# Top-k attention and SoLU feed-forward on one core: a new place table with named PSUM units, small work moved to GpSimd, and the verdict read earlier

## The chip, the core and the metric

The kernel runs on one core of a Trainium2 chip. The metric is the device time of one execution in microseconds, the median of three runs: 1089.7 us (1087.85 to 1089.91). In the profile PE is TensorE, PEld its weight loads, DVE is VectorE, ACT is ScalarE, POOL is GpSimd and SP is SyncE, whose queue issues nearly all DMAs.

## The reference

For 8 batches of 8 heads, with 576 queries and keys of 64 elements, attention keeps the 32 largest scores of each query row:

```python
scores = scale * np.matmul(q, k.transpose(0, 1, 3, 2))
kth = np.partition(scores, -top_k, axis=-1)[..., -top_k:-top_k + 1]
mask = scores >= kth
attn = exp(where(mask, scores, -1e9) - rowmax); attn = attn / (sum + 1e-9); out = attn @ v
```

The result, 4608 tokens of 512 elements, goes through a feed-forward block:

```python
h = x @ w_in                      # 512 -> 1024
sm = exp(h - max) / (sum + 1e-9)
solu = h * sm
ln = (solu - mean(solu)) / np.sqrt(var(solu) + 1e-06) * g_ln
return ln @ w_out                 # 1024 -> 512
```

The weights arrive as 64-bit floats.

## The kernel before, in words

The attention is cut into 32 steps (`steps_of`, L451). A step takes 512 query rows: in the two outer batches (0 and 7) one chunk of 128 queries for all four head pairs, in the others two chunks for two head pairs. Nine rows of work (`j` from 0 to 8) make up a step: eight of 128 queries by 576 keys and one for the queries' tails (64 queries of two heads).

A step runs through these stages. `load_q`, `prep_q` and `prep_qc` fetch the queries and turn them on PE; `load_t` fetches the tails of queries and keys, and `prep_k` turns the keys with their tails. `estimate`, `length`, `root` (L1935) and `gained` guess a threshold for each row from lengths. `scores` (L1980, L1969) multiplies on PE, and `evac` (L1995) copies the result out of PSUM on ScalarE. `count0` and `count1` count the elements above the threshold. From the count, `count_off` (L2106, L2109, GpSimd) makes `far`, the square of how far the count is from 32. On DVE `nearest` (L2064), `best` (L2075) and `merged` (L2092) sort the 16 elements nearest to the threshold; `which` (L2115) compares a table of 16 odd squares, `ranks`, with `far`, `chosen` (L2122) multiplies the sorted elements by the result, and `chosen_sum` (L2125) adds them up: this picks the 32nd largest score. `exps` takes the exponentials on ScalarE, `keep` (L2148) zeroes what lies under the 32nd and sums the rest into `den_all`, `inverse` (L2156, L2160) takes the reciprocals. `transpose_p` and `transpose_last` turn the kept exponentials on PE, `copy_p` (L2249) copies them out, `attn_v` (L2301) and `attn_t` (L2316, L2323) multiply by the values, and `copy_v` (L2338, L2345) scales on DVE.

When a batch's tokens are ready, each of 36 token tiles of 128 rows runs `mm1` (L2356), `hexp` (L2367), `solu` (L2372 to L2379), `square` (L2385), `spread` and `ln` (L2391 to L2398, GpSimd), `transpose_ln`, `copy_ln`, `mm2` (L2420), `store` (L2427: a copy to SBUF) and `send` (L2431: the DMA out). In `solu` the row of exponentials is divided by its sum (the reciprocal `rs` is a scalar operand), and the mean is made by scaling `nmu`.

The 16 weight pieces of 512 KB are brought to 32 bits in the early part: `load_w`, `w_bits` and `w_corr` (DVE), `w_sum` (L1687 to L1692, PE, with three extra matmuls each), `w_copy`. Late in the run they are read once more and tested (`w_again`, `w_exp`, `w_check`). `w_passed` and `w_verdict` (L2451 to L2454) count how many rows met all conditions and write the flag `bad`. After the fast path every engine loads that flag into a register (L2501) and branches (L2503): where the flag is set, a slow general path would run. It does not run for these inputs.

What sets the order is a table written out by hand: `PLACES` gives each piece of work an integer, and `arranged` (L479) sorts the pieces by it. PE, ScalarE, DVE and GpSimd run their instructions in exactly that order; semaphores make each wait for its data and for its buffer. PSUM is handed out by one pool of four units of two banks (`ps_big`, L1536, tag `big`): each of `scores`, `transpose_p`, `attn_v`, `mm1` and the like takes a unit, which is free again when its last reader is through. Which of the four units a take gets is decided by the pool.

## Time and profile before

| | |
|---|---|
| median of three runs | 1089.7 us (1087.85 to 1089.91) |
| profiled execution | 1089.88 us, span 1088.1 us |
| PE busy | 1038.2 us, 95% |
| DVE busy | 998.0 us, 92% |
| ACT busy | 997.0 us, 92% |
| POOL busy | 241.9 us, 22% |

The span runs from the first to the last instruction; the profiled execution's own time lies 1.78 us above it. A busy time is the union of an engine's instructions. PE's matmuls are pipelined and their ends are modelled, so a busy PE is not PE at its peak. "Granted clock" (PEclk) is the TensorE clock that the chip allowed, as a share of 2.4 GHz.

### The profile page before, as it was taken

The numbers are of one execution on the slowest core, as the hardware profiler recorded it, in microseconds if no ns is written. First come the engines' busy times: TensorE is split into PE (matmuls) and PEld (weight loads), VectorE is DVE, ScalarE is ACT, GpSimd is POOL, SyncE is SP. The second block draws the span as 40 slices with busy tenths as digits, with TensorE's granted clock in tenths as the row PEclk, the third lists the DMA queues.
The fourth block names the chain that finished last, engine by engine and source line by source line (L and its number), as shares of the span: only waits on it lengthen the run. The fifth ranks groups of instructions, "written<-read, shape, count | busy, mean of one in ns | idle before, by whom it ended". The sixth has DMA issues, their size and how long they took to land.

```text
span 1088.1 us, 23584 instructions
## 1 busy us (share of the span) xinstructions
PE 1038.2 (95%) x8367; PEld 592.6 (54%) x8367; DVE 998.0 (92%) x2945; ACT 997.0 (92%) x1979; POOL 241.9 (22%) x401
## 2 busy tenths in 40 slices
PE   6858999999999999999999999999999999999997
PEld 3335556554555555565555555565555556565553
DVE  4999998999999999999999999999999999998800
ACT  6968998999999999999999999999999999998722
POOL 1301221313034122122223122221312213220100
PEclk9979999999999999999999999999999999999999
DMA  9510111112111121111210122111310111134301
GB/s 261 160 59 11 41 41 53 44 51 51 52 44 51 36 69 53 32 51 41 73 52 22 51 51 63 41 45 33 79 54 21 41 37 49 54 119 137 108 11 33
DMA packets 108807, 64.54 MB, mean 59 GB/s; under 512 B 87940, under 2 KB 96392, under 8 KB 108680
## 3 DMA queue, kind: packets, MB, share of 16 engines
q1 hardware_dynamic: 107608, 62.68, 20.4%
q8 instruction: 68, 1.11, 0.4%
q14 instruction: 59, 0.48, 0.1%
q10 hardware_dynamic: 1072, 0.26, 0.1%
HBM read 53.35 MB, written 9.57 MB: 58 GB/s over the span
## 4 chain that ended last, share of the span: by engine, by line
PE 57%; DVE 22%; ACT 16%; issue 2%; POOL 1%; DMA 1%; ACTq 0%; DVEq 0%
PE h_ps L2356 16%; PE o_ps L2420 15%; PE om L2301 8%; PE s_ps L1980 6%; DVE w L2064 5%; DVE w L2075 5%; DVE E L2148 4%; PE tp_p L1782 4%; ACT sg L2043 3%; DVE junkv L2000 3%; ACT X L1995 2%; ACT PT L2249 2%; ACT E L2100 2%; PE om L2316 2%; PE s_ps L1969 2%
## 5 line engine op out<-in xcount | busy, mean ns | idle before, releaser
L2420 PE MATMUL o_ps<-w_out,lnT 128*128 128x512 f32 x576 | 261.5, 599 | 1.8 <-ACT lnT L2413 1.0
L2356 PE MATMUL h_ps<-w_in,xTm 128*128 128x512 f32 x512 | 229.8, 598 | 2.7 <-DVE xTm L2338 2.2
L2075 DVE MAX8 w<-w 128x8 f32<-128x288 f32 x576 | 224.7, 445 | 0.0
L2043 ACT ACTIVATE sg<-X,t 128x576 int8<-128x576 f32 x256 | 200.5, 812 | 7.7 <-DVE t L2028 5.5
L2064 DVE SCALAR_TENSOR_TENSOR w<-X,al,sg 128x576 f32<-128x576 f32 x256 | 202.4, 814 | 0.2
L2148 DVE SCALAR_TENSOR_TENSOR E<-X,kth,E 128x576 f32<-128x576 f32 x256 | 201.2, 820 | 1.0 <-ACT E L2100 0.3
L2420 PEld LDWEIGHTS o_ps<-w_out,lnT 128*128 128x128 f32 x576 | 105.4, 190 | 120.9 <-issue 112.6
L2356 PEld LDWEIGHTS h_ps<-w_in,xTm 128*128 128x128 f32 x512 | 94.2, 190 | 110.0 <-issue 105.9
L2000 DVE TENSOR_SCALAR_CACHE_REDUCE junkv<-X,t 128x576 uint8<-128x576 f32 x188 | 148.4, 805 | 6.1 <-ACT X L1995 4.5
L2100 ACT ACTIVATE E<-X 128x1152 f32<-128x1152 f32 x128 | 152.5, 1209 | 0.0
L1995 ACT ACTIVATE X<-s_ps 128x768 f32<-128x768 f32 x192 | 147.2, 839 | 2.0 <-PE s_ps L1980 1.2
L1980 PE MATMUL s_ps<-kT,qT 64*128 64x384 f32 (+1 forms) x1024 | 144.9, 418 | 2.3 <-ACT PT L2249 0.7
L2301 PE MATMUL om<-PT,vm 128*64 128x256 f32 (+3 forms) x1280 | 136.8, 365 | 3.7 <-DVE solu L2375 1.9
L2249 ACT COPY PT<-tp_p 128x1024 f32<-128x1024 f32 x128 | 130.6, 1042 | 0.6 <-PE tp_p L1782 0.3
L1980 PEld LDWEIGHTS s_ps<-kT,qT 64*128 64x128 f32 x1024 | 85.3, 187 | 40.8 <-issue 5.8
L2301 PEld LDWEIGHTS om<-PT,vm 128*64 128x64 f32 x1280 | 82.7, 138 | 45.2 <-ACT PT L2249 4.1
L1935 POOL TENSOR_TENSOR zs<-zs,phalf 128x9 f32<-128x9 f32 x32 | 67.6, 2113 | 137.8 <-DVE zs L1927 118.4
L1782 PE MATMUL tp_p<-ident,E 64*128 64x64 f32 x2048 | 81.4, 224 | 3.9 <-DVE E L2148 1.5
L1782 PEld LDWEIGHTS tp_p<-ident,E 64*128 64x128 f32 x2048 | 72.4, 138 | 21.5 <-issue 5.7
L2036 POOL TENSOR_SCALAR tt<-t 128x9 f32<-128x9 f32 x32 | 18.4, 576 | 288.2 <-DVE t L2028 244.7
L2043 ACT ACTIVATION_READ_ACCUMULATOR sg<-X,t 128x1 f32 x256 | 60.2, 235 | 0.0
L2391 POOL TENSOR_SCALAR var<-var 128x1 f32<-128x1 f32 x36 | 11.0, 306 | 213.0 <-ACT e_sb L2385 207.7
(153 smaller groups left out, 1576.3 us busy)
## 6 DMA issues: line engine op xcount, KB each, us to landing
km<-in_k_dram SPq DMA_DIRECT2D x32, 256.0 KB
vm<-in_v_dram SPq DMA_DIRECT2D x32, 256.0 KB
out_dram<-osb SPq DMA_DIRECT2D x32, 256.0 KB
...
```

The source lines that it names most:

```text
L1782: nc.tensor.transpose(out[:, a, :], part(rows), ident[rows, rows])
L1980: nc.tensor.matmul(out=s[:, n, m * part : (m + 1) * part], lhsT=queries_of(i, t)[hd, :], rhs=kT[hd, k0 : k0 + part], start=True, stop=True,)
L1995: nc.scalar.activation(out=x, in_=s, func=AF.Copy, scale=scale)
L2000: nc.vector.tensor_scalar(out=junk, in0=x_of(i, j), scalar1=st[i][t][:, j : j + 1], scalar2=None, op0=ALU.is_ge, op1=ALU.add, accum_out=co ...
L2043: nc.scalar.activation(out=d["sg", j], in_=x_of(i, j), func=AF.Sign, scale=-(1.0 + 2.0**-23), bias=d["t1"][:, j : j + 1], accum_out=column ...
L2064: nc.vector.scalar_tensor_tensor(out=w, in0=x_of(i, j), scalar=d["al"][:, j : j + 1], in1=d.pop(("sg", j)), op0=ALU.subtract, op1=ALU.mult,)
L2075: nc.vector.max(w8[:, j, 8 * half : 8 * half + 8], w[:, half * SH : (half + 1) * SH])
L2100: nc.scalar.activation(out=d["E", t][:, 0 : x2_of(i, t).shape[1]], in_=x2_of(i, t), func=AF.Exp)
L2148: nc.vector.scalar_tensor_tensor(out=e, in0=x_of(i, j), scalar=d["kth"][:, j : j + 1], in1=e, op0=ALU.is_ge, op1=ALU.mult, accum_out=den_a ...
L2301: nc.tensor.matmul(out=o[h * D : (h + 1) * D, cols], lhsT=vm[:, h, c, :], rhs=pt[:, h * NM + c, :], start=(c == 0), stop=False,)
L2356: nc.tensor.matmul(out=h[:, half, :], lhsT=x[:, c, :], rhs=w_in[:, c, half * 512 : (half + 1) * 512], start=(c == 0), stop=(c == NP - 1),)
L2420: nc.tensor.matmul(out=o, lhsT=d["lnT"][:, c, :], rhs=w_out[:, c, :], start=(c == 0), stop=(c == NF - 1),)
```

## The change

- **Places.** Nearly all places are new. Among the first: a weight piece and the first queries are loaded before keys; `prep_q` and `w_bits` stand before `prep_k`.
- **PSUM units.** The pool of four units is replaced by four pools of one. The string `UNITS` has a character for each take, in the order of the table; `0` to `3` name the unit, `a` to `d` the same four for the takes that only 64-bit weights need.
- **Undivided rows.** `solu` multiplies by the exponentials without the division by their sum. Since a row's scale cancels in the normalization, only the small constant under the root has to be scaled to match: `norm`, three operations on one column on GpSimd, makes that constant and the mean. `square` works on rows scaled by the width, `spread` adds the constant, and the width's power goes into the copy of `g_col`.
- **Ranks on GpSimd.** `which` subtracts `far` from the ranks on GpSimd into a buffer of its own, and `chosen` on DVE tests for zero and multiplies in one instruction.
- **One reciprocal.** `keep` writes its sums in the order in which `inverse` needs them, which is then one instruction.
- **Last tokens and verdict.** The last two token tiles change places. `w_verdict` stands before the last but one half of `mm2`, the flag is loaded just ahead of the last `store`, and the last `send` goes out by ScalarE's queue.

```diff
@@ -468,4 +468,18 @@
+UNITS = (
+    "0b23a1230bc0310231ac3012da123a1231a2badb03120231032120132013cb0210213021321031230123010231"
+    "020320130312032023021321321013120210210321030230131013213213210230123132103210231022031031"
...
+    "103102310230123210"
+)
...
 def order_of_tokens(B):
+    order = [(b, t) for b in range(B) for t in range(NM + b % 2)]
+    return order[:-2] + order[:-3:-1]
...
-    "mm1", "hexp", "solu", "square", "spread", "ln", "transpose_ln", "copy_ln", "mm2", "store", "send",
+    "mm1", "hexp", "solu", "norm", "square", "spread", "ln", "transpose_ln", "copy_ln", "mm2", "store", "send",
...
     "load_k": [
-        0, 1000, 2000, 10400, 36774, 37774, 109467, 119254, 120254, 141054, 208848, 209848, 237397,
...
+        4900, 5900, 10800, 11800, 25850, 26850, 114754, 115754, 119182, 147008, 201104, 210489,
...
-    "load_t": [0, 46136, 142054, 235497, 373816, 520839, 620166, 756840],
+    "load_t": [0, 27850, 148008, 235241, 368859, 514159, 616708, 754927],
     "prep_k": [
-        5218, 7029, 7709, 13812, 108817, 118604, 118987, 140404, 208198, 208581, 234464, 234847,
...
+        10443, 10826, 14811, 15194, 114104, 114487, 118532, 146358, 199863, 209839, 232591, 232974,
...
     "load_q": [
-        3550, 11400, 20200, 29974, 44886, 81424, 124601, 150273, 180902, 220584, 247601, 286809,
...
+        1950, 16700, 35200, 36200, 52123, 84924, 123039, 168135, 187716, 202104, 237481, 272752,
...
     "prep_q": [
-        6558, 19138, 31858, 38406, 80511, 141115, 175499, 179290, 226194, 239634, 288397, 291891,
...
+        4958, 19931, 44587, 44054, 84717, 155005, 175355, 178198, 203970, 254465, 283693, 288241,
...
     "root": [
-        17967, 26053, 40014, 91752, 126126, 153797, 183630, 224113, 249956, 288384, 300353, 327150,
...
+        20469, 27791, 68532, 94941, 127341, 169283, 188046, 202653, 238056, 274637, 296233, 332100,
...
     "mm2": [
...
-        [1058331, 1061873],
...
+        [1054813, 1058355],
     "store": [
...
-        1050731, 1058484, 1065568,
...
+        1047213, 1054966, 1062050,
     "load_w": [
-        4550, 6500, 8450, 12400, 14350, 16300, 18250, 22374, 24324, 26274, 34824, 40524, 42936,
...
+        0, 2950, 6900, 8850, 12800, 14750, 18250, 21950, 23900, 29750, 37200, 39150, 50173, 57175,
...
     "w_bits": [
-        8770, 11064, 13989, 16620, 19315, 23644, 24706, 36870, 32134, 30997, 39887, 45708, 57859,
...
+        4220, 7170, 11120, 13514, 17890, 20274, 25709, 27596, 33137, 34279, 54561, 45672, 57265,
...
-    "w_verdict": [1065308],
+    "w_verdict": [1051221],
@@ -1486,2 +1506,3 @@
     bad: bass.AP,
+    failed: list,
 ):
@@ -1535,3 +1556,3 @@
     )
-    ps_big = ctx.enter_context(tc.tile_pool(name="ps_big", bufs=4, space=PS))
+    ps_big = ctx.enter_context(tc.tile_pool(name="ps_big", bufs=1, space=PS))
 
@@ -1619,4 +1640,6 @@
 
+    units = (str("0123abcd".index(u) % 4) for u in UNITS if w_wide or u in "0123")
+
     def two_banks(name):
-        return ps_big.tile([P, 2, 512], F32, tag="big", name=name)
+        return ps_big.tile([P, 2, 512], F32, tag="big" + next(units), name=name)
 
@@ -1636,3 +1659,5 @@
     def copy_g():
-        nc.scalar.copy(out=g_col, in_=gain["tp"][:, 0:NF])
+        nc.scalar.activation(
+            out=g_col, in_=gain["tp"][:, 0:NF], func=AF.Copy, scale=float(DFF) ** 1.5
+        )
 
@@ -2113,6 +2138,6 @@
         d = st[i]
-        hot = d["hot"] = d["by"][:, 0, :, :]
-        nc.vector.tensor_tensor(
+        hot = d["hot"] = small.tile([P, NT, 16], F32, tag="hot", name="hot", bufs=1)
+        nc.gpsimd.tensor_tensor(
             out=hot, in0=ranks.unsqueeze(1).broadcast_to([P, NT, 16]),
-            in1=d["far"].unsqueeze(2).broadcast_to([P, NT, 16]), op=ALU.is_equal,
+            in1=d["far"].unsqueeze(2).broadcast_to([P, NT, 16]), op=ALU.subtract,
         )
@@ -2121,3 +2146,6 @@
         d = st[i]
-        nc.vector.tensor_tensor(out=d["hot"], in0=d["hot"], in1=d["by"][:, 3, :, :], op=ALU.mult)
+        nc.vector.scalar_tensor_tensor(
+            out=d["hot"], in0=d["hot"], scalar=0.0, in1=d["by"][:, 3, :, :],
+            op0=ALU.is_equal, op1=ALU.mult,
+        )
 
@@ -2147,5 +2175,6 @@
         e = p_of(i, j)
+        row = j if j == 2 * NM else j % 2 * NM + j // 2
         nc.vector.scalar_tensor_tensor(
             out=e, in0=x_of(i, j), scalar=d["kth"][:, j : j + 1], in1=e,
-            op0=ALU.is_ge, op1=ALU.mult, accum_out=den_all[:, i, j : j + 1],
+            op0=ALU.is_ge, op1=ALU.mult, accum_out=den_all[:, i, row : row + 1],
         )
@@ -2155,7 +2184,3 @@
         rden = columns(i, "rden")
-        nc.vector.reciprocal(
-            rden[:, 0 : 2 * NM].rearrange("p (h t) -> p t h", h=2),
-            den_all[:, i, 0 : 2 * NM].rearrange("p (t h) -> p t h", h=2),
-        )
-        nc.vector.reciprocal(rden[:, 2 * NM : NT], den_all[:, i, 2 * NM : NT])
+        nc.vector.reciprocal(rden, den_all[:, i, :])
 
@@ -2353,3 +2378,3 @@
         x = d["x"]()
-        h = once(d, "h", lambda: ps_big.tile([P, 2, 512], F32, tag="big", name="h_ps"))
+        h = once(d, "h", lambda: two_banks("h_ps"))
         for c in range(NP):
@@ -2370,4 +2395,2 @@
 
-        rs = small.tile([P, 1], F32, tag="rs", name="rs")
-        nc.vector.reciprocal(rs, d["sum"])
         d["solu"] = p2.tile([P, DFF], F32, tag="solu", name="solu")
@@ -2375,7 +2398,16 @@
         nc.vector.scalar_tensor_tensor(
-            out=d["solu"], in0=h_of(d), scalar=rs, in1=d["e"], op0=ALU.mult, op1=ALU.mult,
+            out=d["solu"], in0=h_of(d), scalar=1.0, in1=d["e"], op0=ALU.mult, op1=ALU.mult,
             accum_out=nmu,
         )
-        nc.vector.tensor_scalar(
-            out=nmu, in0=nmu, scalar1=-1.0 / DFF, scalar2=None, op0=ALU.mult
+
+    def norm(d):
+
+        less = d["less"] = small.tile([P, 1], F32, tag="less", name="less")
+        nc.gpsimd.tensor_scalar(
+            out=less, in0=d["sum"], scalar1=1e-6 * DFF**3, scalar2=0.0, op0=ALU.mult, op1=ALU.add
+        )
+        nc.gpsimd.tensor_tensor(out=less, in0=less, in1=d["sum"], op=ALU.mult)
+        mean = d["mean"] = small.tile([P, 1], F32, tag="mean", name="mean")
+        nc.gpsimd.tensor_scalar(
+            out=mean, in0=d["nmu"], scalar1=-1.0 / DFF, scalar2=0.0, op0=ALU.mult, op1=ALU.add
         )
@@ -2385,3 +2417,4 @@
         nc.scalar.activation(
-            out=d["e"], in_=d["solu"], func=AF.Square, bias=d["nmu"], accum_out=d["var"]
+            out=d["e"], in_=d["solu"], func=AF.Square, scale=-float(DFF), bias=d["nmu"],
+            accum_out=d["var"],
         )
@@ -2390,5 +2423,3 @@
         var = d["var"]
-        nc.gpsimd.tensor_scalar(
-            out=var, in0=var, scalar1=1.0 / DFF, scalar2=1e-6, op0=ALU.mult, op1=ALU.add
-        )
+        nc.gpsimd.tensor_tensor(out=var, in0=var, in1=d["less"], op=ALU.add)
         d["rstd"] = small.tile([P, 1], F32, tag="rstd", name="rstd")
@@ -2398,3 +2429,3 @@
         nc.gpsimd.tensor_scalar(
-            out=d["solu"], in0=d["solu"], scalar1=d["nmu"], scalar2=d["rstd"],
+            out=d["solu"], in0=d["solu"], scalar1=d["mean"], scalar2=d["rstd"],
             op0=ALU.add, op1=ALU.mult,
@@ -2425,2 +2456,7 @@
     def store(d):
+        if d is tokens[-1]:
+            failed.append(nc.values_load(
+                bad[0:1, 0:1], min_val=0, max_val=1,
+                skip_runtime_bounds_check_because="a comparison's result",
+            ))
         d["osb"] = p1.tile([P, DM], F32, tag="osb", name="osb")
@@ -2429,4 +2465,5 @@
     def send(d):
+        queue = nc.scalar if d is tokens[-1] else nc.sync
         for rows, dst in d["stores"]:
-            nc.sync.dma_start(out=dst, in_=d["osb"][rows, :])
+            queue.dma_start(out=dst, in_=d["osb"][rows, :])
 
@@ -2439,3 +2476,3 @@
             (zk_all, 1e-12, ALU.is_gt), (den_all, 1.0, ALU.is_ge), (den_all, 1e15, ALU.is_le),
-            (sum_all, 1.0, ALU.is_ge), (sum_all, 1e30, ALU.is_le), (w_ok, 128.5, ALU.is_le),
+            (sum_all, 1.0, ALU.is_ge), (sum_all, 1e12, ALU.is_le), (w_ok, 128.5, ALU.is_le),
             (end_all, 0.5, ALU.is_gt),
@@ -2481,3 +2518,3 @@
         keep, inverse, spread_r, copy_s, turn_r, copy_r, rd_out, rd_in, transpose_p, copy_p, transpose_last, copy_last, attn_v, attn_t,
-        copy_v, mm1, hexp, solu, square, spread, ln, transpose_ln, copy_ln, mm2, store, send, load_g, turn_g,
+        copy_v, mm1, hexp, solu, norm, square, spread, ln, transpose_ln, copy_ln, mm2, store, send, load_g, turn_g,
         copy_g, load_w, w_bits, w_corr, w_sum, w_copy, w_gain, w_again, w_exp, w_check, w_passed,
@@ -2499,6 +2536,5 @@
     bad = keep.tile([1, 1], I32, tag="bad", name="bad")
-    fast_path(tc, *args, bad)
-    failed = nc.values_load(bad[0:1, 0:1], min_val=0, max_val=1,
-                            skip_runtime_bounds_check_because="a comparison's result")
-    with tc.If(failed > 0):
+    failed = []
+    fast_path(tc, *args, bad, failed)
+    with tc.If(failed[0] > 0):
         general_path(tc, *args)
```

## Rows read from the trace of the kernel before

**Rows 1.** The page, part 1: busy us, share of the span, instructions

```profile
PE 1038.2 (95%) x8367; PEld 592.6 (54%) x8367; DVE 998.0 (92%) x2945; ACT 997.0 (92%) x1979; POOL 241.9 (22%) x401
```

**Rows 2.** The page, part 4: shares of the chain that ended last

```profile
PE 57%; DVE 22%; ACT 16%; issue 2%; POOL 1%; DMA 1%; ACTq 0%; DVEq 0%
```

**Rows 3.** Timeline of POOL: start us, us, engine, line, operation; first `root`

```profile
22.71 2.01 POOL L1935 TENSOR_TENSOR zs<-zs,phalf 128x9 f32<-128x9 f32 x1 [20.36 <-DVE zs L1927]
```

**Rows 4.** Timeline of ACT: three of the 36 `store` copies

```profile
164.63 0.75 ACT L2427 COPY osb<-o_ps 128x512 f32<-128x512 f32 x1
...
206.48 0.60 ACT L2427 COPY osb<-o_ps 128x512 f32<-128x512 f32 x1
...
1080.45 0.59 ACT L2427 COPY osb<-o_ps 128x512 f32<-128x512 f32 x1 [6.28 <-PE o_ps L2420]
```

**Rows 5.** Groups of DVE by line: count, busy us, mean ns, idle before

```profile
L2148 DVE SCALAR_TENSOR_TENSOR E<-X,kth,E 128x576 f32<-128x576 f32 x256 | 201.2, 820 | 1.0 <-ACT E L2100 0.3 <-issue 0.2
...
L2115 DVE TENSOR_TENSOR by<-ranks,far 128x144 f32<-128x144 f32 x32 | 9.7, 302 | 0.0
...
L2372 DVE RECIPROCAL rs<-sum_all 128x1 f32<-128x1 f32 x36 | 5.6, 156 | 16.9 <-ACT e_sb L2367 16.6
...
L2379 DVE TENSOR_SCALAR nmu<-nmu 128x1 f32<-128x1 f32 x36 | 5.5, 154 | 1.3
...
L2160 DVE RECIPROCAL rden<-den_all 128x1 f32<-128x1 f32 x32 | 3.6, 112 | 0.0
```

**Rows 6.** One line each: ns min/median/max, first and last start

```profile
L2109 POOL TENSOR_TENSOR far<-far x32: 201/518/1175, 50.1 to 1005.3; 128x9 f32<-128x9 f32 x32
...
L2148 DVE SCALAR_TENSOR_TENSOR E<-X,kth,E x256: 796/814/1680, 71.8 to 1025.1; 128x576 f32<-128x576 f32 x128
```

**Rows 7.** Timeline of POOL, then of DVE, 690 to 720 us

```profile
693.56 0.60 POOL L2109 TENSOR_TENSOR far<-far 128x9 f32<-128x9 f32 x1
702.24 0.26 POOL L2391 TENSOR_SCALAR var<-var 128x1 f32<-128x1 f32 x1 [8.08 <-ACT e_sb L2385]
...
703.13 0.31 DVE L2122 TENSOR_TENSOR by<-by 128x144 f32<-128x144 f32 x1
```

**Rows 8.** Waits of PE: waited for, us in total, times, longest

```profile
PE om L2301 <- DVE solu L2375: 1.9, 1, 1.9
```

**Rows 9.** Stretches: us, busy us by engine (instructions), PEclk, DMA share, GB/s

```profile
55.00:60.00 5.00, 0.00 (x0) 0.00 (x0) 5.00 (x11) 4.99 (x14) 0.00 (x0) 0.50 0.00 0
70.00:75.00 5.00, 2.72 (x28) 1.65 (x27) 5.00 (x15) 3.24 (x6) 0.00 (x0) 1.00 0.28 107
180.00:182.00 2.00, 2.00 (x18) 1.68 (x16) 2.00 (x7) 0.72 (x2) 1.11 (x2) 0.50 0.29 83
```

**Rows 10.** Timeline of PE, 176 to 188 us

```profile
179.16 4.07 PE L2301 MATMUL om<-PT,vm 128*64 128x128 f32 x32 [1.86 <-DVE solu L2375]
...
185.46 1.92 PE L2301 MATMUL om<-PT,vm 128*64 128x128 f32 x32
```

**Rows 11.** Timeline of PE, then of DVE, from the start

```profile
9.30 0.37 PE L1782 MATMUL tp_k<-ident,qk_tails 64*128 64x64 f32 x1 [2.39 <-DMA qk_tails<-in_k_dram]
...
11.44 0.17 DVE L1856 TENSOR_TENSOR stats<-sums,heads 128x6 bf16<-128x6 f32 x1 [9.22 <-ACT kT L1834]
```

**Rows 12.** Stretches of the start, columns as in rows 9

```profile
0.00:10.00 10.00, 1.40 (x11) 0.96 (x11) 1.19 (x8) 1.49 (x2) 1.79 (x37) 1.00 0.94 181
10.00:20.00 10.00, 10.00 (x63) 5.77 (x63) 5.91 (x14) 9.30 (x31) 0.00 (x0) 1.00 1.06 324
```

**Rows 13.** Flag load L2501, branch L2503: ns min/median/max, first and last start

```profile
L2501 SPq TENSOR_LOAD <-bad x1: 841/841/841, 1082.3 to 1082.3; - x1
...
L2503 SPq EVENT_SEMAPHORE  x8: 17/17/17, 1086.1 to 1086.7; - x8
L2503 ACTq COMPARE_BRANCH  x1: 54/54/54, 1081.4 to 1081.4; - x1
...
L2503 ACTq EVENT_SEMAPHORE  x1: 17/17/17, 1085.7 to 1085.7; - x1
```

More of the change, by code (lines that the diff above doesn't have):

```diff
@@ new lines @@
+        [99561, 108898],
+        [136125, 146234],
+        [158968, 171847],
+        [193719, 187748],
+        [225810, 221745],
+        [258577, 262835],
+        [287807, 287116],
+        [319273, 313968],
+        [341060, 347114],
+        [375505, 374721],
+        [394747, 404333],
+        [433489, 422728],
+        [461074, 454078],
+        [487820, 486491],
+        [511202, 530372],
+        [540945, 557314],
+        [584352, 599472],
+        [614624, 625790],
+        [642165, 651531],
@@ L1175 @@
[L1175 to L1181 removed]
+        [79248, 70794],
+        [100489, 109753],
+        [140208, 146918],
+        [159683, 173991],
+        [196779, 188257],
+        [227369, 222218],
+        [261004, 263314],
+        [289217, 287589],
+        [331756, 314426],
+        [343175, 347821],
+        [380868, 375287],
+        [395641, 407160],
@@ new lines @@
+        [438124, 423117],
+        [461768, 454462],
+        [489483, 487106],
+        [517584, 533829],
+        [543006, 557698],
+        [585187, 600016],
+        [619356, 626947],
+        [643425, 652285],
+        [677583, 685877],
+        [705391, 720086],
+        [736646, 752993],
+        [769067, 779376],
+        [803785, 813463],
+        [843237, 851534],
+        [861094, 866315],
+        [896755, 902651],
+        [914529, 921776],
+        [941932, 949178],
+        [971559, 991104],
@@ new lines @@
+        [204661, 207452],
+        [228989, 226695],
+        [272545, 278767],
+        [291317, 288602],
+        [336466, 341609],
+        [370200, 368422],
+        [387129, 395790],
+        [413815, 416019],
+        [450800, 449022],
+        [471445, 469667],
+        [506146, 508350],
+        [535068, 537859],
+        [581118, 596771],
+        [609072, 611276],
+        [637109, 639313],
+        [666754, 664976],
+        [695597, 693339],
+        [721435, 723639],
+        [749580, 757818],
@@ new lines @@
+        [294754, 294200],
+        [339942, 344856],
+        [373544, 374006],
+        [394151, 398338],
+        [419145, 419607],
+        [454255, 453793],
+        [475147, 474740],
+        [511560, 512022],
+        [538537, 540687],
+        [587948, 599319],
+        [614383, 614845],
+        [641915, 642377],
+        [670621, 670204],
+        [700277, 696538],
+        [726241, 726703],
+        [753454, 760366],
+        [784784, 785246],
+        [829641, 836229],
+        [859132, 864401],
@@ new lines @@
+        [437525, 434090],
+        [441069, 444504],
+        [488421, 475964],
+        [501741, 498306],
+        [541546, 549361],
+        [558845, 553766],
+        [566491, 563056],
+        [616051, 619486],
+        [628438, 631982],
+        [674105, 677540],
+        [686535, 681945],
+        [727402, 732445],
+        [736918, 744725],
+        [791286, 786124],
+        [803391, 799956],
+        [812825, 807905],
+        [870022, 866587],
+        [877001, 873566],
+        [909753, 913188],
```

864 lines of the change are left out of this document (382 added, 482 removed), and 576 rows, old and new, of the table PLACES.

## The prediction

> **What bounds the kernel now.** I read the busy shares first, then the chain of waits, then single starts. TensorE is busy 1038.2 of 1088.1 us, VectorE 998.0, ScalarE 997.0 [rows 1]: three engines are nearly full, so no one of them can be relieved alone. The chain that ended last lies 57% on PE, 22% on DVE, 16% on ACT [rows 2]. The reader should see from this that work taken from DVE is worth at most about a fifth of its length, and that PE, from which the change takes nothing, goes on setting the end.
>
> The next view is that of single starts. Each engine runs its instructions in the order of the place table. The integers in it behave as nanoseconds: the first square root of GpSimd (`root`, place 17,967) starts at 22.71 [rows 3]; the copies `store` with places 159,179, 197,741 and 1,065,568 start at 164.63, 206.48 and 1080.45 [rows 4]. The lag of start behind place is 4.74, 5.45, 8.74 and 14.88 us. So the trace tells of a table with three separate losses: 4.74 us at the start, 3.29 us in one jump between 164 and 206, and 6.85 us spread over the rest (under 1% of the span). A new table is not believed for its own sake; I take over its differences only with these measured losses, and bound them where a row can.
>
> **The change part by part.**
>
> *Order and DVE work.* Off DVE go the reciprocal `rs` (36 x 156 ns = 5.6 us), the scaling of `nmu` (36 x 154 ns = 5.5), the comparison with `ranks` (32 x 302 ns = 9.7) and one of two reciprocals (32 x 112 ns = 3.6) [rows 5]: 24.4 us. `chosen` keeps its 144 elements and one pass. Worth from both sides: 24.4 us if DVE alone set the time, nothing if PE did; by DVE's 22% of the chain, 5.4. The new table puts the last `store` at 1,062,050 in place of 1,065,568, which is 3.52 us earlier. I take 3.5, which lies between nothing and 5.4. PE keeps every matmul; the end of the table is again mm1, transposes and mm2 without a gap.
>
> *GpSimd.* It gains 32 subtractions of 144 elements and 36 x 3 operations on one column (`norm`); `spread` keeps its two. A 9-element operation there takes 201 to 1175 ns [rows 6]. I take 0.6 us for a subtraction and 0.25 us for a column operation: 32 x 0.6 + 108 x 0.25 = 46 us beside 242 us busy, 27% of the span. What hides the subtraction: in a typical step `far` is ready at 694.16 (693.56 + 0.60) and its first reader's successor `chosen` starts at 703.13 on DVE, with GpSimd idle for 8.08 us between [rows 7]. What hides `norm`: ScalarE's square of the same token runs beside it, and the next GpSimd operation, `var`, is the one that waits for that square [rows 7]. If this cover went, a token's `ln` would come 0.8 us later, at a PE that is then in another token's matmuls. Both engines share a cost: `keep` on DVE has a median of 814 ns, a mean of 820 and a maximum of 1680 [rows 5, 6], so meetings with GpSimd cost DVE (820 - 814) x 256 = 1.5 us in all. With 140 more operations on about 400 I charge 1 us, bounds 0 and 5.
>
> The Trainium skill ("SBUF — State Buffer", Who interferes with whom) speaks against this move: a DVE instruction with two SBUF inputs and a GpSimd instruction that reads SBUF contend, and whoever issues second blocks fully. The maximum of 1680 ns agrees that it happens; the mean says that mostly GpSimd is the one that waits. As a loss to DVE the rule is rival C.
>
> *PSUM units.* Before, a pool hands out four units. In the trace PE waited 1.9 us at the `om` of 179.16 for DVE's `solu` [rows 8], which reads another token's unit: the place of that `om` was 171,764 and of `solu` 172,010, so the order had not meant them to share. The table names a unit for each of 738 takes, and in it each unit's last reader stands before the next taker. This wait goes; what `om` waits for next is the copy that frees its own unit, which the table puts earlier. And it cost more than 1.9 us: right behind the idle time the granted clock was 0.50 (1.2 GHz) [rows 9], and the 32 matmuls took 4.07 us where the same 32 took 1.92 at 2.4 GHz a little later [rows 10]. Idle and slow matmuls are the jump of 3.29 us. If no such gap recurs I gain 3.3; if one does, nothing; below nothing, if there are two. I take 3.3: after 110 us the new places leave PE no gap over 1.4 us.
>
> *Start.* Before, PE's first matmuls wait for the tails until 9.30, and DVE has no data work until 11.44 [rows 11]. Now a weight piece (512 KB) and the first queries (256 KB) are issued first, and `prep_q` (place 4,958) and `w_bits` (4,220) come before `prep_k` (10,443), which is the first to need tails and keys. The DMA engines moved 181 GB/s in the first 10 us and 324 in the next [rows 12]. Up to `prep_q` 0.79 MB and the tails' 0.26 are wanted: 1.05 MB / 181 GB/s = 5.8 us, a lag of 0.8. Up to `prep_k` of the first keys (another weight piece and one pair's keys more) it is 1.84 MB: 10.1 us, ahead of its place. So transfers allow a lag of 0.5 to 1; the engines before had 4.74. I take 1.8, bounds 0.5 and 4.74 (nothing gained). What is late then is the order itself: DVE's chain of weight pieces.
>
> *Low clock early.* Between 55 and 60 us PE was empty and the clock 0.50 [rows 9]. The new places leave a hole of 5 us at 52, so this can recur; it fell where PE had nothing to do, and I cost it at nothing, with rival B as its other end.
>
> *End.* In the kernel before, the flag is read after the last `store`: SyncE loads it from 1082.3 on for 841 ns, branches, and shows its next instruction at 1086.1; ScalarE branches at 1081.4 and goes on at 1085.7 [rows 13]. From the start of the last copy to the end of the span are 1088.1 - 1080.45 = 7.65 us. After the change `w_verdict` stands 11 us before the end, so GpSimd, DVE and SyncE load and branch early. SyncE's sends are past by then. The load waits on each queue for the flag; behind it stand on ScalarE the last copy and the send, which wait longer for PE, on PE and DVE nothing. The last path is copy 0.59, the issue of one send on ScalarE about 0.5, its branch 4.3 (1081.4 to 1085.7), and up to 2.0 of closing on SyncE: 6.4 to 7.4. I take 6.65, a gain of 1.0; bounds: a gain of 2.3 if the jump takes SyncE's 3.0 us (1086.1 - 1082.3 - 0.84), or a loss of 0.5 if a load stands in front of the copy.
>
> *Sum.* Last `store`: 1062.05 + 1.8 + 6.85 = 1070.7. With the end 6.65 and 1 us for GpSimd: span 1078.35. The profiled execution took 1089.88 for a span of 1088.1, so 1.78 more: 1080.1. The median of the runs is 0.2 below that execution: **1080 us**, 0.9% faster.
>
> **Rivals.**
> A, only the order's difference arrives: the start lags 4.74 again, another stall with low clock comes in place of the removed one, the end keeps its 7.65 (the units only rename what the pool did). 1062.05 + 14.88 + 7.65 + 1.78 = 1086.4. For it: losses of this sort have been in every stretch of the trace. Against: two of them have a named cause that is gone.
> B, slower: the clock stays low into dense work. The place is 46 to 80 us, where PE gets sparse weight sums before the first dense attention work (place 67,198). At 0.50 the 32 matmuls took 2.12 times as long, so 13 us of dense work at that clock loses 13 x (1 - 1/2.12) = 6.9. With A's losses: 1093. It decides from about 10 us of dense work on. Against it: before, with the same hole, the clock was back at 1.00 in 70 to 75, when the attention work began [rows 9].
> C, slower: meetings with GpSimd block DVE, not GpSimd. At 1680 - 814 = 0.87 us for each of 140 operations, 122 us of DVE; times 22%, 27 us: 1107. It decides from one meeting in three on. Against it: the mean of 820.
>
> **How the numbers follow.** Forecast 0.70 (1075 to 1084), A 0.18 (to 1088), little or nothing left 0.07, B 0.03, C 0.02. Low end: start 0.5, end 5.3, no cost on GpSimd, 6.0 for the rest: 1062.05 + 6.5 + 5.3 + 1.8 = 1075.6, taken as 1075. High end: A with 1 us for GpSimd, 1087.4. A measurement here tells 0.2% (2.2 us) from no change: faster 0.87, same 0.08, slower 0.05.
>
> **What would show it.** Right: the lag of `store` behind its place is 2 to 3 us at the first token and 8 to 10 at the last; no wait of `om` for `solu`, and the clock at 1.00 from 100 us to the last matmul; DVE's busy time about 24 us less; GpSimd's about 45 more; SyncE's load of the flag done before the last copy. Wrong: a first lag near 5 (start), a stretch at 0.50 behind a PE gap (units), a mean of `keep` over 850 ns (GpSimd), over 7.4 us from last copy to end. The prediction as a whole is wrong if the last `store` starts after 1078.

## Result and profile after

The median of four runs is 1076.03 us (1075.49 to 1076.51). The ratio to the kernel before is 0.9879, 95% interval 0.9861 to 0.9896: 13.6 us less, where 9.7 were forecast (1089.7 to 1080). The profiled execution took 1075.49 us for a span of 1073.7, so the 1.8 us around the span are unchanged and the span tells the rest.

The page of the kernel after, part 1 (beside [rows 1]):

```profile
PE 1038.0 (97%) x8367; PEld 593.4 (55%) x8367; DVE 984.7 (92%) x2809; ACT 995.8 (93%) x1979; POOL 287.6 (27%) x541
```

PE's work is the same; the span shrank around it. The chain that ended last, after (beside [rows 2]):

```profile
PE 64%; ACT 23%; DVE 7%; issue 3%; DMA 2%; POOL 1%; SPq 0%; ACTq 0%; DVEq 0%; POOLq 0%
```

DVE's share fell from 22% to 7%. The first `root` and the `store` copies, after: a row of POOL's timeline, then the one-line view of the copies (ns min/median/max, first and last start).

```profile
21.83 1.93 POOL L1960 TENSOR_TENSOR zs<-zs,phalf 128x9 f32<-128x9 f32 x1 [19.47 <-DVE zs L1952]
...
L2463 ACT COPY osb<-o_ps x36: 558/587/884, 132.5 to 1067.9; 128x512 f32<-128x512 f32 x36
```

The places, in us, are 20.47 (`root`) and 131.18 and 1062.05 (first and last copy). The lag, start less place, is 1.4 at `root`, 1.3 at the first copy and 5.8 at the last ([rows 3, 4]: 4.7 and 14.9; before, the first copy has place 132.18 and started at 137.3, a lag of 5.1). From these views the whole gain in span can be booked. Its first row is read off the two tables and was known beforehand; what the run adds is that the lag did not eat it up.

| term | before | after | gain, us |
|---|---|---|---|
| place of the last copy | 1065.57 | 1062.05 | 3.5 |
| lag at the first copy | 5.1 | 1.3 | 3.8 |
| growth of the lag from there to the last copy | 9.8 | 4.5 | 5.3 |
| last copy to the end of the span | 7.7 | 5.8 | 1.8 |
| span | 1088.1 | 1073.7 | 14.4 |

Where the growth went is seen in the stretches of the kernel after (columns as in [rows 9]):

```profile
39.00:42.00 3.00, 3.00 (x6) 0.93 (x6) 3.00 (x7) 3.00 (x10) 0.00 (x0) 0.50 0.76 203
56.00:62.00 6.00, 4.85 (x8) 1.91 (x9) 5.86 (x18) 6.00 (x16) 0.31 (x1) 0.50 0.28 87
70.00:75.00 5.00, 4.58 (x54) 2.77 (x52) 5.00 (x14) 4.59 (x7) 3.80 (x5) 1.00 0.00 0
180.00:182.00 2.00, 2.00 (x20) 1.23 (x19) 2.00 (x11) 2.00 (x6) 0.00 (x0) 1.00 0.08 14
100.00:1060.00 960.00, 952.45 (x7802) 548.61 (x7798) 894.60 (x2567) 911.39 (x1798) 268.07 (x477) 1.00 0.19 53
```

The low clock is left only in the sparse early part; from 100 us on the clock is 1.00 and PE lacks 7.55 of 960 us. The two largest entries among the waits of PE in that stretch (in total, times, longest) are below 1 us; `om` for `solu` [rows 8] is gone.

```profile
PE s_ps L2005 <- ACT PT L2274: 0.9, 1, 0.9
PE tp_p L1807 <- ACT X L2020: 0.9, 2, 0.7
```

The start: PE's and DVE's first data work, and the first stretch (beside [rows 11, 12]).

```profile
6.46 0.69 PE L1807 MATMUL tp_qk<-ident,q_sb 64*128 64x64 f32 x8 [6.46 <-DMA q_sb<-in_q_dram]
...
4.81 0.43 DVE L1688 TENSOR_SCALAR w_tmp<-w_raw 128x512 uint32<-128x512 uint32 x1 [2.61 <-DMA w_raw<-in_moe_w_in_dram]
...
0.00:10.00 10.00, 3.54 (x13) 1.63 (x14) 4.76 (x15) 2.57 (x4) 1.79 (x37) 1.00 0.94 195
```

PE starts 2.8 us earlier and DVE 6.6, at nearly the same DMA rate (195 GB/s against 181): mainly what comes first changed, not how fast it comes. The moved operations (groups: count, busy us, mean ns, idle before), and `keep` as one line:

```profile
L2177 DVE SCALAR_TENSOR_TENSOR E<-X,kth,E 128x576 f32<-128x576 f32 x256 | 199.7, 817 | 3.5 <-ACT E L2125 3.0
...
L2147 DVE SCALAR_TENSOR_TENSOR hot<-hot,by 128x144 f32<-128x144 f32 x32 | 9.7, 303 | 0.7
...
L2140 POOL TENSOR_TENSOR hot<-ranks,far 128x144 f32<-128x144 f32 x32 | 18.3, 573 | 1.8
L2411 POOL TENSOR_SCALAR mean<-nmu 128x1 f32<-128x1 f32 x36 | 14.2, 395 | 25.9 <-DVE solu L2398 24.3 <-DVE hit L2481 0.8 <-DVE zs L1952 0.8
...
L2177 DVE SCALAR_TENSOR_TENSOR E<-X,kth,E x256: 752/812/1593, 66.5 to 1013.0; 128x576 f32<-128x576 f32 x128
```

With GpSimd 45.7 us busier, `keep` has a mean of 817 ns, not more than before (820). The end, flag load and branch (beside [rows 13]):

```profile
L2458 SPq TENSOR_LOAD <-bad x1: 845/845/845, 1063.3 to 1063.3; - x1
...
L2539 SPq EVENT_SEMAPHORE  x8: 17/17/17, 1066.9 to 1071.0; - x8
...
L2539 SPq COMPARE_BRANCH  x1: 45/45/45, 1064.2 to 1064.2; - x1
...
L2539 ACTq COMPARE_BRANCH  x1: 62/62/62, 1069.1 to 1069.1; - x1
L2539 ACTq EVENT_SEMAPHORE  x1: 17/17/17, 1072.8 to 1072.8; - x1
```

SyncE branches at 1064.2 and is at its next instruction at 1066.9, before the last copy (1067.9). The last path is the copy, the send, and ScalarE's branch with 3.7 us to its next instruction.

### The profile page after: what moved, and what is told of

Read it like the earlier page. It is cut to its first block, busy times and chain, and to the rows that moved or that the text cites. A ratio compares the mean times of both kernels' runs of the same rounds, so it can differ in the third digit from the quotient of the medians.

```text
span 1073.7 us, 23585 instructions
## 1 busy us (share of the span) xinstructions
PE 1038.0 (97%) x8367; PEld 593.4 (55%) x8367; DVE 984.7 (92%) x2809; ACT 995.8 (93%) x1979; POOL 287.6 (27%) x541
## 4 chain that ended last, share of the span: by engine, by line
PE 64%; ACT 23%; DVE 7%; issue 3%; DMA 2%; POOL 1%; SPq 0%; ACTq 0%; DVEq 0%; POOLq 0%
PE o_ps L2451 19%; PE h_ps L2381 16%; PE om L2326 8%; PE s_ps L2005 7%; ACT sg L2068 5%; PE tp_p L1807 4%; ACT X L2020 4%; ACT PT L2274 3%; ACT E L2125 3%; ACT junka L2033 2%; PE s_ps L1994 2%; PE om L2341 2%; PE tp_pt L1807 1%; PE tp_ln L1807 1%; DVE E L2177 1%
## 5 line engine op out<-in xcount | busy, mean ns | idle before, releaser
L2125 ACT ACTIVATE E<-X 128x1152 f32<-128x1152 f32 x128 | 154.9, 1223 | 0.3 <-PE tp_p L1807 0.3
L2020 ACT ACTIVATE X<-s_ps 128x768 f32<-128x768 f32 x192 | 149.5, 859 | 0.4 <-PE s_ps L2005 0.2
L2005 PE MATMUL s_ps<-kT,qT 64*128 64x192 f32 (+1 forms) x1024 | 146.3, 418 | 3.3 <-ACT PT L2274 1.3
L2274 ACT COPY PT<-tp_p 128x1024 f32<-128x1024 f32 x128 | 133.6, 1059 | 1.8 <-PE tp_p L1807 1.6
L2061 POOL TENSOR_SCALAR tt<-t 128x9 f32<-128x9 f32 x32 | 14.9, 467 | 288.0 <-DVE t L2053 235.9
L1807 PEld LDWEIGHTS tp_p<-ident,E 64*128 64x128 f32 x2048 | 75.0, 139 | 25.0 <-issue 8.0
L1807 PE MATMUL tp_p<-ident,E 64*128 64x64 f32 x2048 | 83.8, 225 | 1.7 <-ACT X L2020 0.9
L2068 ACT ACTIVATION_READ_ACCUMULATOR sg<-X,t 128x1 f32 x256 | 62.5, 244 | 0.0
L2398 DVE SCALAR_TENSOR_TENSOR solu<-h_ps,e_sb 128x1024 f32<-128x1024 f32 x36 | 43.7, 1214 | 18.5 <-ACT e_sb L2392 18.0
```

The source lines that it names most:

```text
L1807: nc.tensor.transpose(out[:, a, :], part(rows), ident[rows, rows])
L2005: nc.tensor.matmul(out=s[:, n, m * part : (m + 1) * part], lhsT=queries_of(i, t)[hd, :], rhs=kT[hd, k0 : k0 + part], start=True, stop=True,)
L2020: nc.scalar.activation(out=x, in_=s, func=AF.Copy, scale=scale)
L2068: nc.scalar.activation(out=d["sg", j], in_=x_of(i, j), func=AF.Sign, scale=-(1.0 + 2.0**-23), bias=d["t1"][:, j : j + 1], accum_out=column ...
L2125: nc.scalar.activation(out=d["E", t][:, 0 : x2_of(i, t).shape[1]], in_=x2_of(i, t), func=AF.Exp)
L2274: nc.scalar.copy(out=dst, in_=tp)
```

## Experiments

Each run gives a median, a ratio to the kernel before as timed beside it (medians of 1089.2 to 1090.2), and the same bookkeeping. The medians come from four to ten executions, the lags from one, the profiled one. "Over after" is against the 1076.0 of the result. The theory was the prediction's, corrected by the table above: four separate causes (start order, named units, a lighter DVE that the new places need, the end). The rivals are told with each run. "Growth" is the lag of the last copy less that of the first; "end" the span less the last copy's start.

| run | kernel | median us | ratio, 95% interval | first lag | last lag | growth | end | DVE busy |
|---|---|---|---|---|---|---|---|---|
| | before | 1089.6 | | 5.1 | 14.9 | 9.8 | 7.7 | 998.0 |
| | after | 1076.0 | 0.9879 (0.9861 to 0.9896) | 1.3 | 5.8 | 4.5 | 5.8 | 984.7 |
| 1 | after, pool of four | 1082.4 | 0.9937 (0.9915 to 0.9959) | 4.1 | 12.3 | 8.2 | 5.8 | 985.9 |
| 2 | before, named units | 1084.7 | 0.9963 (0.9949 to 0.9977) | 4.3 | 9.6 | 5.3 | 7.6 | 998.1 |
| 3 | after, old start order | 1080.1 | 0.9920 (0.9904 to 0.9937) | 5.3 | 9.6 | 4.3 | 5.6 | 984.7 |
| 4 | after, old arithmetic | 1087.2 | 0.9984 (0.9975 to 0.9994) | 3.0 | 18.0 | 15.0 | 4.8 | 1003.4 |
| 5 | before, new arithmetic | 1086.8 | 0.9971 (0.9958 to 0.9983) | 5.2 | 11.2 | 6.0 | 7.7 | 986.2 |
| 6 | after, old end | 1077.1 | 0.9878 (0.9861 to 0.9894) | 3.3 | 7.4 | 4.1 | 6.3 | 985.1 |
| 7 | before, all but places | 1083.7 | 0.9944 (0.9927 to 0.9961) | 5.2 | 10.7 | 5.5 | 5.6 | 985.9 |
| 8 | after, old `solu` only | 1081.6 | 0.9924 (0.9907 to 0.9940) | 1.9 | 11.6 | 9.7 | 4.8 | 995.4 |
| 9 | after, old ranks only | 1077.6 | 0.9894 (0.9877 to 0.9910) | 3.3 | 9.2 | 5.9 | 4.8 | 991.7 |
| 10 | after, no `ends` | 1076.0 | 0.9883 (0.9866 to 0.9899) | 1.9 | 5.9 | 4.0 | 5.7 | 983.6 |
| 11 | after, shorter searches | 1075.3 | 0.9867 (0.9850 to 0.9883) | 3.3 | 6.8 | 3.5 | 5.6 | 969.9 |
| 12 | before, shorter searches | 1083.8 | 0.9952 (0.9935 to 0.9968) | 2.8 | 8.1 | 5.3 | 7.7 | 984.8 |

**1. The units undone.**

```diff
-    ps_big = ctx.enter_context(tc.tile_pool(name="ps_big", bufs=1, space=PS))
+    ps_big = ctx.enter_context(tc.tile_pool(name="ps_big", bufs=4, space=PS))
-        return ps_big.tile([P, 2, 512], F32, tag="big" + next(units), name=name)
+        return ps_big.tile([P, 2, 512], F32, tag="big", name=name)
```

> The changed kernel with the pool of four units back in place of the table of units; all else as changed (1076.0 us). Theory (the pool lets two tiles share a unit that the order did not mean to, PE waits for a foreign reader, and a wait over a microsecond brings a low clock behind it): 1078 to 1082 us, PE waits of 0.5 to 2 us for solu, evac or copy_p that the changed kernel does not show, and perhaps a stretch at clock 0.50 after 100 us. Rival (the table only renames what the pool does anyway): 1076 us, within 1 us, with the same waits as the changed kernel.

6.4 us over after, 0.4 above the theory's band. The waits of PE from 100 to 1060 us hold again such as the table had taken out:

```profile
PE tp_qk L1807 <- DVE xTt L2370: 2.0, 2, 1.6
PE s_ps L2005 <- DVE solu L2398: 1.2, 2, 0.9
```

The rename-only rival falls. Of the 6.4 us the growth shows 3.7. Another 2.8 stand at the first copy, but they were there at the first `root` already, and run 11, which names the units, was as late there. In both, DVE waited for the DMA of the third weight piece and got it over 1 us later than in the kernel after (DVE in after, run 1 and run 11, then POOL in runs 1 and 11):

```profile
13.24 0.43 DVE L1688 TENSOR_SCALAR w_tmp<-w_raw 128x512 uint32<-128x512 uint32 x1 [2.30 <-DMA w_raw<-in_moe_w_in_dram]
14.41 0.43 DVE L1688 TENSOR_SCALAR w_tmp<-w_raw 128x512 uint32<-128x512 uint32 x1 [2.27 <-DMA w_raw<-in_moe_w_in_dram]
14.63 0.43 DVE L1688 TENSOR_SCALAR w_tmp<-w_raw 128x512 uint32<-128x512 uint32 x1 [1.92 <-DMA w_raw<-in_moe_w_in_dram]
24.55 1.94 POOL L1960 TENSOR_TENSOR zs<-zs,phalf 128x9 f32<-128x9 f32 x1 [22.20 <-DVE zs L1952]
24.78 1.92 POOL L1960 TENSOR_TENSOR zs<-zs,phalf 128x9 f32<-128x9 f32 x1 [22.43 <-DVE zs L1952]
```

So these 2.8 are not shown to be the pool's. The clock stayed 1.00 behind these waits, of which the longest took 1.6 us: that a wait of over a microsecond brings the low clock, as the theory had it, is not borne out.

**2. Units alone, in the old places.** The string names for each take the unit that is free longest in the old order.

```diff
+UNITS = (
...
-        return ps_big.tile([P, 2, 512], F32, tag="big", name=name)
+        return ps_big.tile([P, 2, 512], F32, tag="big" + next(units), name=name)
```

> The kernel before with nothing changed but the units: each of its 738 takes gets, by a table worked out from its own places, the unit that was freed longest ago. Theory: the jump of 3.3 us between 164 and 206 us goes (no wait of om for solu at 179, clock 1.00 there) and up to 2 us of the lag that is spread over the rest: 1084.5 to 1086.5 us. Rival (the stall only moves, or it came from DVE being late with solu): 1089 to 1090 us, with a PE gap of 1 to 2 us somewhere else between 100 and 300 us.

4.9 us faster; in the growth 4.5, of which 3.3 are the jump at 179 us. The copies with places 159.18 and 197.74, between which the lag jumped before, now lag by 4.60 and 4.64. These two, then the stretch that was at 0.50 in [rows 9]:

```profile
163.78 0.75 ACT L2442 COPY osb<-o_ps 128x512 f32<-128x512 f32 x1
202.38 0.59 ACT L2442 COPY osb<-o_ps 128x512 f32<-128x512 f32 x1
...
180.00:182.00 2.00, 2.00 (x38) 1.74 (x38) 2.00 (x6) 2.00 (x4) 1.81 (x3) 1.00 0.59 162
```

**3. The old start order.** The first loads get the places that they had (keys first, then queries, then weights).

```diff
     "load_k": [
-        4900, 5900, 10800, 11800, 25850, 26850, ...
+        0, 1000, 2000, 10400, 25850, 26850, ...
     "load_q": [
-        1950, 16700, ...
+        3550, 16700, ...
     "load_w": [
-        0, 2950, 6900, 8850, 12800, ...
+        4200, 6500, 8450, 12350, 12800, ...
```

> The changed kernel with the loads of the start issued in the order of the kernel before (keys of three pairs, then queries, then the weight pieces); the engines' order is as changed. Theory (what is late at the start is carried to the end, since DVE and ScalarE have no slack behind it): the lag of start behind place is 4 to 5.5 us at 100 us instead of 1.3, and the run takes 1079 to 1080.5 us. Rival (the hole around 52 us and the sparse stretch up to 66 us absorb it): the lag is back under 2 us by 100 us, and the run takes 1076 to 1077 us.

4.0 us over after; all its executions (1079.1 to 1081.1) lie above all of after (1075.5 to 1076.5). The first lag is 5.3 and the growth, 4.3, is nearly that of after (4.5): the late start is carried to the end almost whole.

**4. The old arithmetic in the new places.** `which` and `chosen`, `solu` and both reciprocals as before, on DVE; no `norm`.

```diff
-        nc.gpsimd.tensor_tensor(
+        nc.vector.tensor_tensor(
...
-            out=d["solu"], in0=h_of(d), scalar=1.0, in1=d["e"], op0=ALU.mult, op1=ALU.mult,
+            out=d["solu"], in0=h_of(d), scalar=rs, in1=d["e"], op0=ALU.mult, op1=ALU.mult,
```

> The changed kernel with the arithmetic of the kernel before (the comparison with the ranks on DVE, the reciprocal and the scaling of the mean on DVE, two reciprocals per step), in the new places: DVE gets its 24 us back, GpSimd loses 46. Theory (PE sets the end, DVE is 7 to 22 per cent of the chain): 1078 to 1081.5 us. Rival (DVE sets the pace, and its relief is the largest part of the gain): 1086 to 1100 us.

11.1 us over after, nearly the kernel before: the rival. The growth is 15.0, and the chain that ended last runs through DVE:

```profile
DVE 46%; PE 34%; ACT 12%; issue 4%; POOL 1%; DMA 1%; ACTq 0%; SPq 0%; DVEq 0%; POOLq 0%
```

**5. The new arithmetic in the old places.**

```diff
-        nc.vector.tensor_tensor(
+        nc.gpsimd.tensor_tensor(
...
+    "norm": [
```

> The kernel before with the new arithmetic alone (ranks on GpSimd right behind the count's square, undivided rows, one reciprocal per step); places, pool and end as before. Theory (in any order PE waits less if DVE has 24 us less to do; DVE is 22 per cent of the chain before): 1083 to 1086.5 us. Rival (an order written for the old costs has its waits on other engines and on units, and cannot use the relief): 1088 to 1090 us, with DVE idle 20 us longer.

2.8 us faster, between the two. DVE is 11.8 us less busy, but PE got a new wait, for `ln`, now later on GpSimd, beside the old one (waits from 100 to 1060 us):

```profile
PE tp_ln L1789 <- POOL solu L2411: 1.8, 1, 1.8
PE om L2308 <- DVE solu L2380: 1.5, 1, 1.5
```

**6. The old end.** The flag is loaded behind the last store by every engine, and SyncE sends the last rows; `w_verdict` keeps its new place.

```diff
-        queue = nc.scalar if d is tokens[-1] else nc.sync
+        queue = nc.sync
+    failed.append(nc.values_load(bad[0:1, 0:1], min_val=0, max_val=1,
+                                 skip_runtime_bounds_check_because="a comparison's result"))
```

> The changed kernel with the end of the kernel before: the flag is loaded after the last store, on every engine, and the last send goes out by SyncE. Theory (the load and the jump of SyncE come back behind the last copy): 7.4 to 7.8 us from the start of the last copy to the end of the span instead of 5.8, and 1077.4 to 1078.4 us. Rival (the end is set by the landing of the last send, in either form): 5.8 to 6.3 us and 1076 to 1076.5 us.

The theory's size missed: the end is 6.3, not 7.4 to 7.8, and the time is 1.0 over after with a ratio that can't be told from it. The end lies in the rival's band, the time 0.6 above it. SyncE's and ScalarE's loads:

```profile
L2534 ACTq TENSOR_LOAD <-bad x1: 471/471/471, 1069.4 to 1069.4; - x1
L2534 SPq TENSOR_LOAD <-bad x1: 513/513/513, 1070.4 to 1070.4; - x1
```

SyncE loads 1.0 us after the start of the last copy (1069.4); in the kernel before it was 1.9 [rows 4, 13]. So 1.4 of the gain at the end come with what this run keeps (the early verdict, the order of the last tokens), and 0.5 with the early load and ScalarE's send. The runs with the whole new end in the new places have ends from 4.8 to 5.8, so the 0.5 is not firm.

**7. Everything but the places.** Runs 2 and 5 together, with the new end.

```diff
-    "w_verdict": [1065308],
+    "w_verdict": [1054000],
```

> The kernel before with the table of units of its own places, the new arithmetic and the new end together; places as before, but for the verdict. Theory (the parts add up: 4.5 us for the units, 3 to 5 for the arithmetic, 1.8 for the end): 1078 to 1081 us, so that 2 to 5 us are left to the new places. Rival (the arithmetic is worth nothing without places made for it): 1082.5 to 1084 us, and 6 to 8 us are left to the places.

The rival's band. Growth 5.5 is no better than with the units alone, since a stall came back: PE waited for `ln`, and a stretch at 0.50 followed (a timeline row of PE, then a stretch):

```profile
263.54 0.71 PE L1805 MATMUL tp_ln<-ident,solu 64*128 64x64 f32 x16 [2.02 <-POOL solu L2427]
...
265.00:268.00 3.00, 3.00 (x37) 2.59 (x35) 3.00 (x8) 2.49 (x5) 1.89 (x1) 0.50 0.02 5
```

The places are worth the remaining 7.6 us: 3.5 of table length, 3.9 of first lag, 1.0 of growth, less 0.2 at the end make 8.2, the difference of the spans (1081.9 to 1073.7). The units that the new table names and the swap of the last tokens are counted with the places here.

**8. Old `solu` only, in the new places.**

```diff
+        nc.vector.reciprocal(rs, d["sum"])
...
+        nc.vector.tensor_scalar(
+            out=nmu, in0=nmu, scalar1=-1.0 / DFF, scalar2=None, op0=ALU.mult
```

> The changed kernel with the old token arithmetic alone (reciprocal and scaling of the mean on DVE, 11.1 us of its 24.4), ranks as changed. Theory (it is the amount of DVE work that counts): about half of the 11 us that the whole old arithmetic cost, 1080.5 to 1083 us. Rival (it is the delay of square and of the freeing of the PSUM unit that counts, 0.3 us in each of 36 token chains): 1084 to 1087 us, nearly the whole 11 us.

5.6 us over after (5.2 in the growth): the theory's band, below the rival's. The chain:

```profile
PE 49%; DVE 32%; ACT 13%; issue 3%; DMA 1%; POOL 0%; ACTq 0%; SPq 0%; DVEq 0%; POOLq 0%
```

**9. Old ranks only.**

```diff
-        nc.gpsimd.tensor_tensor(
+        nc.vector.tensor_tensor(
-            in1=d["far"].unsqueeze(2).broadcast_to([P, NT, 16]), op=ALU.subtract,
+            in1=d["far"].unsqueeze(2).broadcast_to([P, NT, 16]), op=ALU.is_equal,
```

> The kernel after, with only the comparison with the ranks back on DVE (32 operations of 144 elements, 9.7 us by the rows of before). Theory (in the new places each microsecond of DVE work costs about half a microsecond, as the solu arithmetic did: 5.6 us for 11.1 us): 4 to 5 us over the kernel after, 1080 to 1081, and with the solu arithmetic the two make up the 11.1 us that the old arithmetic cost as a whole. Rival (the comparison is off the bound, since far is ready long before, and only solu's path counts): 1076 to 1078. A second rival (the GpSimd subtraction was itself a burden, so taking it off GpSimd gives back what DVE loses): 1075 to 1077 with GpSimd about 20 us less busy.

1.5 us over after (1.4 in the growth), not 4 to 5: the theory's fixed price per microsecond falls. The second rival falls too: GpSimd is 19.4 us less busy, and the run is no faster. Runs 8 and 9 together do not make up run 4 (7.1 of 11.1; run 4 has the second reciprocal as well). The chain is still PE's:

```profile
PE 63%; ACT 15%; DVE 10%; issue 2%; POOL 1%; DMA 0%; SPq 0%; ACTq 0%; POOLq 0%; DVEq 0%
```

**10. `ends` left out.**

```diff
-        nc.vector.tensor_tensor(
-            out=end_all[:, i, :], in0=w8[:, :, 7], in1=w8[:, :, 15], op=ALU.max
-        )
+        if i == 0:
+            nc.gpsimd.memset(end_all, 0.0)
```

> The kernel after, with 5.6 us of DVE work left out (the 32 maxima of 9 elements in `ends`; the condition on them is left out of the verdict). It asks whether DVE still bounds the kernel after the change. Theory (DVE's share of the chain fell from 22 to 7 per cent, so DVE has been relieved enough; more relief is worth 5.6 x 0.07 = 0.4 us): 1075.3 to 1076.5. Rival (each microsecond of DVE work is still worth half a microsecond, as when work is added): 1073 to 1074.

No gain, as the theory had it, but DVE's busy time fell by 1.1 us only, so the run alone decides nothing.

**11 and 12. Shorter searches, in either kernel.**

```diff
-                w8[:, j, 8 * half : 8 * half + 8], w[:, half * SH : (half + 1) * SH]
+                w8[:, j, 8 * half : 8 * half + 8], w[:, half * SH : half * SH + 256]
```

> The kernel after, in which each of the 576 searches of `best` on DVE reads 256 of its 288 elements (the last 32 columns of each half are left out of the candidates, and the verdict's two conditions on them are void). At the 444 ns that a search of 288 took this should shorten DVE by about 32/288 of 256 us, some 20 to 28 us, on its busy time too, since these are long instructions. Leaving out 5.6 us of short ones took only 1.1 us off DVE's busy time, so that run could not tell. Theory (after the change DVE is no longer the bound; its share of the chain is 7 per cent): at most 2 us faster than after, 1074 to 1076. Rival (each microsecond of DVE work is worth about half, in both directions): 10 us or more, 1063 to 1067.

> The same edit in the kernel before: DVE shorter by 20 to 28 us in the old places, with the old arithmetic. Theory (a lighter DVE can only give back the lag behind the old places, and the stall at 179 us goes with it, as in the run with the new arithmetic alone): 3 to 6 us faster than before, 1084 to 1087. Rival (DVE's 22 per cent of the chain is a lower bound and the old table could have run faster with a lighter DVE): 10 us or more, below 1080.

DVE's busy time fell by 14.8 us in the one and 13.2 in the other (the expected 20 to 28 was too much: a search went from 444 to 414 ns). The time fell by 0.7 us in the kernel after, where the ratios can't be told apart, and by 5.8 in the kernel before (against the median of the table; 1083.8 lies 0.2 below the theory's band). So both theories stand. Of the lag that run 12 lost, 4.5 us are in the growth; 2.3 stand at the first copy, and 1.2 of these at the first `root`, before any search. In the kernel before the relief alone cut the jump at 179 us from 3.3 to 1.2: `om` still waited 1.4 us, but the clock stayed. A group of DVE in run 11; then, from run 12, the wait, the stretch and the copies with places 159.18 and 197.74:

```profile
L2100 DVE MAX8 w<-w 128x8 f32<-128x256 f32 x576 | 205.9, 414 | 0.1
...
PE om L2301 <- DVE solu L2375: 1.4, 1, 1.4
...
180.00:182.00 2.00, 2.00 (x42) 1.87 (x40) 0.69 (x2) 2.00 (x4) 0.69 (x1) 1.00 0.60 211
...
162.30 0.76 ACT L2427 COPY osb<-o_ps 128x512 f32<-128x512 f32 x1
202.02 0.60 ACT L2427 COPY osb<-o_ps 128x512 f32<-128x512 f32 x1
```

## Why the prediction was right, and which terms were off

The time lies in the forecast range because two causes were named rightly in the main, the start and the stall. The sum was too slow: the span was forecast as 1078.35 and came out at 1073.7. Of these 4.65 us, 2.4 lie in the rest of the lag, 1.0 in GpSimd, 0.8 in the end and 0.4 in the start. Of the prediction's signs, the lags (2 to 3 at the first token, 8 to 10 at the last) came out below, at 1.3 and 5.8, and DVE's 24 us did not come; the others held.

**Places and DVE: 3.5 taken, with the wrong reason for the size.** The 3.5 is the difference of two numbers of the tables, so no run could miss it; the forecast bounded it by 24.4 us of DVE work times 22% of the chain. Runs 4, 8 and 9 show no such price. In the new places DVE work is worth 1.5 us for the first 7.0 us of busy time that come back, 5.6 for 10.7 (of `solu`, which stands ahead of a token's `ln`) and 11.1 for 18.7; below what the kernel after has, nearly nothing (run 11). I read this as a table cut to an engine that has just enough room. These runs move work off GpSimd too, and those with the old `solu` (4 and 8) make each token's chain longer; how much is DVE's load and how much the longer chain they do not separate.

**DVE's busy time fell 13.3 us, not 24.** The records of short instructions lie over one another, as in these two of the kernel before, where the second starts 0.08 us before the first ends:

```profile
700.72 0.15 DVE L2379 TENSOR_SCALAR nmu<-nmu 128x1 f32<-128x1 f32 x1
700.79 0.36 DVE L2092 TENSOR_TENSOR by<-w 128x72 f32<-128x72 f32 x2
```

All DVE records added up fell by 29.7 us (1218.0 to 1188.3), their union by 13.3. Count times mean duration, as in [rows 5], overprices a short instruction: in run 10 it made 5.6 us out of 1.1.

**Start: 2.9 forecast, 3.4 at `root`, 3.8 at the first copy, in these two traces.** Here the trace of the kernel after is a lucky one. In the eight traces with its start order (after, runs 1, 4, 6 and 8 to 11) the lag at `root` runs from 1.4 to 4.3, mean 2.7; in the six with the old order it runs from 3.6 to 5.2, mean 4.4. So the taken 1.8 was hit within a spread that nobody had forecast, and between the means the order is worth 1.7; run 3 (5.2) and the kernel after (1.4) are the two ends. The prediction let the transfers allow a lag of 0.5 to 1 and put what is late down to DVE's order; the traces point to the transfers. In all eight DVE waited for the third weight piece, got it between 13.24 and 14.63 us, and the lag at `root` rose with that time. Run 3 confirms that a late start is carried.

**Stall and low clock: 3.3 forecast, and gone.** But the units are not the only cure: each of runs 2, 5 and 12 lost the stretch at 0.50 in the old places, two of them with the pool of four. The cause was the meeting of `om` with a late `solu`. An own unit ends the wait (run 2); with a lighter DVE it stayed, at 1.5 and 1.4 us (runs 5 and 12), but no low clock followed. So the gains of the parts overlap: taken back one at a time, units, start order, arithmetic and end cost 6.4, 4.0, 11.1 and 1.0, together 22.5 for a change of 13.6. With only the 3.7 of the growth for the units it is still 19.8.

**The rest of the lag: "6.85 spread over the rest" was taken over unchanged; this step failed.** After, from `root` to the last copy, it is 4.4 (5.8 less 1.4), 2.4 us less: the largest share of the missed 4. From the third copy, behind the jump, to the last the lag grew by 6.1 us before, by 5.0 in run 2 and by 3.8 in run 12: named units or a lighter DVE each take some of the small waits. The kernel after has both, and 4.5 from its first copy to its last.

**GpSimd: 1 us forecast, nothing found.** Its busy time rose 45.7 us (46 forecast), partly by luck: the new groups take 52.0 (a column operation 0.31 us, not 0.25), other groups 6.3 less than before. `keep` is stretched in single cases only. The longest took 1593 ns and started while GpSimd's `ln` ran, as did each of the four over 900 ns; `ln` was there before the change (DVE, then POOL):

```profile
452.42 0.81 DVE L2177 SCALAR_TENSOR_TENSOR E<-X,kth,E 128x576 f32<-128x576 f32 x1
...
453.15 1.59 DVE L2177 SCALAR_TENSOR_TENSOR E<-X,kth,E 128x576 f32<-128x576 f32 x1
452.19 1.95 POOL L2429 TENSOR_SCALAR solu<-solu,mean,rstd 128x1024 f32<-128x1024 f32 x1
```

The Trainium skill ("SBUF — State Buffer", Who interferes with whom) has it that a DVE instruction with two SBUF inputs and a GpSimd instruction that reads SBUF contend, and that the one that issues second is blocked. The trace agrees in part: the `ln` started first, but so it did for the `keep` at 452.42, which took its usual 0.81 us. The mean of 817 says that such meetings cost no more than before. Rival C fell with it.

**End: 1.0 forecast, 1.8 measured.** ScalarE's branch took 3.7 us instead of 4.3 and the closing 0.9 instead of up to 2.0. The branch varies with the same code (below), so its part is not firm.

**Rivals A and B.** The last lag is 5.8, not 14.9; the early low clock was there (in 39 to 42 and 56 to 62 us) but over by 70 us.

No version tried beats the kernel after: run 11 leaves part of the search out, and run 10 changes nothing measurable.
